# Transposing q, k and the attention output by DMA instead of identity matmuls, in a kernel of linear attention and an MLP

## The chip, the cores and the metric

The kernel runs on one core of a Trainium2 chip. The metric is the time of one execution on the device in microseconds (us), as the median of several runs. A run more than 1.5% above the fastest of its kernel counts as slow and is left out of comparisons. Ratios of two kernels are the mean time of one kernel's fast runs over that of the other's in the same rounds, so they are not quite the ratio of the medians quoted beside them.

Engine names in the profile: PE is TensorE, PEld its weight loads, DVE VectorE, ACT ScalarE, POOL GpSimd, SP the sync engine whose queue issues most DMAs. A DMA has landed when its data have arrived; landing times count from the issue.

## The reference, cut to what matters

```python
# q, k, v: (8, 8, 576, 64) f32; omega: (128, 64); w_in: (512, 2048); w_out: (2048, 512)
def phi(x):                                   # random features
    h = einsum('bhsd,md->bhsm', x, omega) - sum(x*x)/2
    return exp(h - max(h)) / sqrt(128)
q_p, k_p = phi(q * 64**-0.25), phi(k * 64**-0.25)
kv  = einsum('bhsm,bhsd->bhmd', k_p, v);  z = sum(k_p, axis=s)
att = (q_p @ kv) / (q_p @ z + 1e-6)
x   = att.transpose(0, 2, 1, 3).reshape(4608, 512)
h   = x @ w_in;  g = h * clip(h + 3, 0, 6) / 6;  out = g @ w_out
```

## The kernel before

One batch of attention is four pairs of heads. For each pair, q, k and v (288 KB each) are loaded as f32, q and k are cast to bf16 on POOL, and side by side they give 9 blocks of 128x128 that this kernel transposes, so that the head dimension, over which its K and Q matmuls contract, lies on partitions. The kernel before does it with a matmul against an identity and an eviction from PSUM:

```python
def e_T(E, cs=cs, vT=vT):                     # 4 blocks = one unit; 9 units per batch
    for i, c in enumerate(cs):
        src = qkb[(b * NP + c // NR) % 3][:, c % NR, :, :].rearrange("p t d -> p (t d)")
        ins = E.matmul(ring.t[vT.slot][:, 128*i:128*i+128], src, ident[:], start=True, stop=True)
    return ins
...                                           # eviction on DVE or ACT into qkT, then K and Q matmuls
op("POOL", 1.3, lambda E: E.tensor_tensor(    # v scaled by 1/max, both head halves on POOL
    vbd[u2][p0:p1, :, f0:f0 + 64], v32[u3][p0:p1, :, :], cbc, ALU.mult), ...)
...                                           # kv and num matmuls, then xb = num / den
def e_x(E):                                   # the attention output, transposed in the same way
    for t_ in range(4):
        ins = E.matmul(ring.t[vx.slot][:, 128*t_:128*t_+128], xb[pb][:, pr, 128*t_:128*t_+128],
                       ident[:], start=True, stop=True)
    return ins
...                                           # eviction into xT; e_S does the same for 64 left-over rows per batch, into xS
```

The MLP then takes blocks of 512 tokens: `mm1` (xT by wi, 64 matmuls of 512 columns a block, then the activation on ACT and DVE) and `mm2` (by wo, 64 matmuls). Attention of batch b runs while PE does mm1 of block b-1 and mm2 of block b-2.

All instructions go through a small list scheduler that runs when the program is built. It has a cost in us for each operation and fixes the order on every engine. At run time each engine works through its own list in order and waits on semaphores; an instruction that waits holds everything behind it on that engine (in `dma_only` below, a cast on POOL waits 4.70 us and the v scaling listed behind it starts only after it).

The softmax here doesn't subtract the row's maximum and nothing guards it: scores larger than these inputs give would overflow.

## Time and profile before

The time was 363.59 us (363.31 to 364.85). The span of the profiled run, 361.9 us, divides as follows; a block starts where the timeline of PEld shows its first weight load of mm1 (the first of each 64).

| stretch of before | from, us | to, us | length, us |
|---|---|---|---|
| head, to the first matmul of mm1 | 0 | 35.7 | 35.7 |
| blocks 0 and 1 | 35.7 | 97.0 | 61.3 |
| blocks 2 to 6, five periods of 38.2 | 97.0 | 287.9 | 190.9 |
| tail, MLP alone | 287.9 | 361.9 | 74.0 |

These are the groups of the page that the change removes or moves. The columns are line, engine, operation, output from input, shape, count, then busy us and mean ns of one, then idle time of the engine just before them and what ended it.

```profile
L462 POOL TENSOR_TENSOR vbd<-v,cc 64x576 bf16<-64x576 f32 x64 | 73.7, 1152 | 45.0 <-DVE cc L457 30.6
L401 PE MATMUL p<-ident,qkb 128*128 128x128 bf16 x288 | 28.6, 231 | 4.3 <-POOL qkb L379 3.7
L319 ACT CAST qkT<-p 128x512 bf16<-128x512 f32 x41 | 24.1, 590 | 14.0 <-PE p L401 13.4
```

The head and one period as windows (from, to and length in us; busy us and count of PE, PEld, DVE, ACT, POOL; granted clock, DMA share, GB/s). The DMA share adds up packet times over 16 engines and can pass 1 (1.03 in the first row):

```profile
0.00:35.70 35.70, 22.41 (x227) 16.22 (x228) 21.59 (x47) 19.76 (x38) 26.28 (x43) 0.90 1.03 298
135.20:173.40 38.20, 38.14 (x307) 21.54 (x306) 25.49 (x47) 25.36 (x47) 16.30 (x24) 1.00 0.44 121
```

The v scaling on POOL takes 1.15 us for a half.

### The profile page before, as it was taken

To read this page: it belongs to the slowest core of one execution; us is meant where nothing else is said; L and a number is where in the kernel's file an instruction comes from. 1 tells how busy PE (TensorE), PEld (TensorE's weight loads), DVE (VectorE), ACT (ScalarE), POOL (GpSimd) and SP (SyncE) were. 2 spreads that over 40 slices of the span, in tenths; PEclk is the share of its full clock that TensorE was granted. 3 is DMA by queue.
4 is the path that set the end of the run, shared out by engine and by line. 5 is a ranking of instruction groups with operands and counts; after the bars stand their busy time and mean duration, and the time that the engine had idled before them with its cause. 6 is when DMAs were issued, how large, how long until landed. Compare 5 with 4: busy or idle time off the path is not lost.

```text
span 361.9 us, 6522 instructions
## 1 busy us (share of the span) xinstructions
PE 342.1 (95%) x2569; PEld 189.3 (52%) x2569; DVE 222.0 (61%) x406; ACT 211.2 (58%) x383; POOL 137.4 (38%) x206
## 2 busy tenths in 40 slices
PE   3677998999999999999999999999999999999994
PEld 2545565456555655565556555655555544444442
DVE  3676997588558655776567656865687534333411
ACT  3684985575476747584767657674867443444400
POOL 3897596346026621663056505570344100000000
PEclk9898999999999999999999999999999999999999
DMA  7999699635234531645155513322110121121123
GB/s 254 346 279 309 158 223 240 200 95 161 72 94 127 168 115 37 187 130 159 31 145 175 161 29 99 92 55 70 31 29 2 31 58 29 31 54 33 31 60 85
DMA packets 23981, 42.39 MB, mean 117 GB/s; under 512 B 2960, under 2 KB 7056, under 8 KB 23952
## 3 DMA queue, kind: packets, MB, share of 16 engines
q1 hardware_dynamic: 19728, 37.79, 35.8%
q0 software_dynamic: 4224, 4.19, 7.2%
q8 instruction: 20, 0.33, 0.4%
q14 instruction: 9, 0.07, 0.1%
HBM read 36.73 MB, written 9.44 MB: 128 GB/s over the span
## 4 chain that ended last, share of the span: by engine, by line
PE 80%; POOL 11%; DVE 3%; ACT 2%; issue 1%; DMA 1%; SPq 0%; POOLq 0%
PE p L556 32%; PE p L532 30%; POOL vbd L462 7%; PE p L473 4%; PE p L416 4%; PE p L401 4%; PE p L411 3%; PE p L488 2%; POOL qkb L379 2%; PE p L507 1%; DVE mx L429 1%; ACT kp L422 1%; POOL vbd L465 1%; DMA qk<-in_k_dram 1%; ACT qpT L425 1%
## 5 line engine op out<-in xcount | busy, mean ns | idle before, releaser
L539 DVE SCALAR_TENSOR_TENSOR gT<-tsb,p 128x512 bf16<-128x512 bf16 x144 | 98.6, 685 | 80.3 <-ACT tsb L537 78.5
L556 PE MATMUL p<-wo,gT 128*128 128x512 bf16 x576 | 145.2, 379 | 0.5 <-ACT kp L422 0.5
L537 ACT ACTIVATE tsb<-p 128x512 bf16<-128x512 f32 x144 | 86.3, 599 | 89.3 <-PE p L532 89.1
L532 PE MATMUL p<-xT,wi 128*128 128x512 bf16 x512 | 130.4, 379 | 0.1
L462 POOL TENSOR_TENSOR vbd<-v,cc 64x576 bf16<-64x576 f32 x64 | 73.7, 1152 | 45.0 <-DVE cc L457 30.6
L556 PEld LDWEIGHTS p<-wo,gT 128*128 128x128 bf16 x576 | 54.6, 98 | 57.6 <-ACT kp L422 0.7
L379 POOL CAST qkb<-qk 128x576 bf16<-128x576 f32 x64 | 42.7, 668 | 87.7 <-PE p L401 80.1
L532 PEld LDWEIGHTS p<-xT,wi 128*128 128x128 bf16 x512 | 47.1, 98 | 45.0 <-DVE gT L539 0.9
L429 DVE TENSOR_REDUCE mx<-kp 128x4 f32<-128x512 bf16 x72 | 49.0, 681 | 8.4 <-ACT kp L422 8.0
L422 ACT ACTIVATE kp<-p 128x512 bf16<-128x512 f32 x72 | 43.0, 598 | 12.7 <-PE p L416 11.9
L425 ACT ACTIVATE qpT<-p 128x512 bf16<-128x512 f32 x72 | 43.1, 599 | 1.0 <-PE p L411 0.3
L401 PE MATMUL p<-ident,qkb 128*128 128x128 bf16 x288 | 28.6, 231 | 4.3 <-POOL qkb L379 3.7
L319 ACT CAST qkT<-p 128x512 bf16<-128x512 f32 x41 | 24.1, 590 | 14.0 <-PE p L401 13.4
L416 PE MATMUL p<-omk,qkT 128*128 128x128 bf16 x288 | 28.8, 224 | 1.7 <-DVE qkT L320 0.9
L401 PEld LDWEIGHTS p<-ident,qkb 128*128 128x128 bf16 x288 | 21.8, 104 | 14.4 <-POOL qkb L379 3.2
L411 PE MATMUL p<-qkT,omq 128*128 128x512 bf16 x72 | 28.3, 393 | 0.0
L473 PE MATMUL p<-vbd,kp 128*128 128x130 bf16 x288 | 23.0, 226 | 4.6 <-POOL vbd L465 3.9
L416 PEld LDWEIGHTS p<-omk,qkT 128*128 128x128 bf16 x288 | 20.2, 100 | 13.5 <-ACT qkT L319 4.4
L500 DVE TENSOR_TENSOR xb<-p,rec 128x640 bf16<-128x640 f32 x32 | 26.2, 819 | 0.3
L320 DVE CAST qkT<-p 128x512 bf16<-128x512 f32 x31 | 21.3, 686 | 6.1 <-PE p L401 6.1
L473 PEld LDWEIGHTS p<-vbd,kp 128*128 128x128 bf16 x288 | 18.5, 100 | 10.6 <-POOL vbd L465 7.3
L319 ACT COPY osb<-p 128x512 f32<-128x512 f32 x31 | 18.3, 589 | 8.5 <-PE p L556 8.5
(35 smaller groups left out, 160.7 us busy)
## 6 DMA issues: line engine op xcount, KB each, us to landing
qk<-in_q_dram SPq DMA_DIRECT2D x32, 288.0 KB, 3.3
qk<-in_k_dram SPq DMA_DIRECT2D x32, 288.0 KB, 3.9
v<-in_v_dram SPq DMA_DIRECT2D x32, 288.0 KB, 3.1
out_dram<-osb SPq DMA_DIRECT2D x72, 128.0 KB, 2.4
wi<-in_moe_w_in_dram POOLq DMA_DIRECT2D x4, 512.0 KB, 11.8
wo<-in_moe_w_out_dram POOLq DMA_DIRECT2D x4, 512.0 KB, 8.2
om<-in_omega_dram SPq DMA_DIRECT2D x1, 32.0 KB, 1.7
```

The costliest lines, as they stand in the source:

```text
L379: op("POOL", 0.65, lambda E, which=which, u3=u3, u2=u2: E.tensor_copy(qkb[u2][:, :, which, :], qk32[u3][:, which, :].rearrange("p (r d) -> ...
L401: ins = E.matmul(ring.t[vT.slot][:, 128 * i:128 * i + 128], src, ident[:], start=True, stop=True)
L416: ins = E.matmul(ring.t[vK.slot][:, 128 * i:128 * i + 128], qkT_r.t[vqk.slot][:, i, :], omk[:], start=True, stop=True)
L422: op("ACT", actt(512), lambda E, u=u, vK=vK: E.activation(kp[pb][:, 4 * u:4 * u + 4, :].rearrange("p c m -> p (c m)"), ring.t[vK.slot], AF ...
L425: op("ACT", actt(512), lambda E, u=u, vQ=vQ: E.activation(qpT[pb][:, :, 4 * u:4 * u + 4, :].rearrange("m h c p -> m c h p"), ring.t[vQ.slo ...
L429: op("DVE", dvet(512), lambda E, u=u: E.reduce_max(mx[pb][:, 4 * u:4 * u + 4], kp[pb][:, 4 * u:4 * u + 4, :], axis=AX.X), pos(u) + 0.03, r ...
L462: op("POOL", 1.3, lambda E, p0=p0, p1=p1, f0=f0, cbc=cbc: E.tensor_tensor(vbd[u2][p0:p1, :, f0:f0 + 64], v32[u3][p0:p1, :, :], cbc, ALU.mu ...
L473: ins = E.matmul(ring.t[vkv.slot][:, 0:130], kp[pb][:, c0 + r, :], vbd[u2][:, r, :], start=(r == 0), stop=(r == NR - 1))
L532: ins = E.matmul(h_ps[hu], wi[:, c, 128 * f:128 * f + 128], xv[:, c, :], start=(c == 0), stop=(c == NJ - 1))
L537: op("ACT", actt(512), lambda E: E.activation(tsb[tu][:], h_ps[hu], AF.Relu, bias=0.5, scale=1.0 / 6.0), t - 0.1, reads=[("h", hu)], write ...
L539: op("DVE", dvet(512), lambda E: E.scalar_tensor_tensor(gT[gu][:, f, :], tsb[tu][:], 1.0, h_ps[hu], ALU.min, ALU.mult), t - 0.1, reads=[(" ...
L556: ins = E.matmul(ring.t[vo.slot], gT[gu][:, f, 128 * tc:128 * tc + 128], wo[:, f, :], start=(f == 0), stop=(f == NF - 1))
```

## The change

The intent is to take work off TensorE, the bound, and give it to DMA engines that are less than half busy in the middle (share 0.44 in the period above). Its core:

```diff
-    qkT_r = Ring([sbt("qkT%d" % u, [128, 4, 128], BF16) for u in range(3)])
+    qkT = [sbt("qkT%d" % u, [128, NR, 128], BF16) for u in range(4)]
...
-                   t0 - 0.2, writes=[(key, u3)], ...)                       # loads of q, k (and v)
+                   t0 - 0.2, reads=[("wi", pr)] if b == 1 else [], writes=[(key, u3)], ...)
...
-                op("POOL", 0.65, lambda E, ...: E.tensor_copy(qkb..., qk32...), ...)
+                op(EV_C, {"POOL": 0.70, "ACT": actt(576), "DVE": dvet(576)}, evac(...), ...)
+            op("SP", 1.0, lambda E, u2=u2: E.dma_start_transpose(
+                qkT[gp % 4][:], qkb[u2][:].rearrange("p r t d -> p (r t d)")), ...)
...
-            op("PE", 4 * mmt(128), e_T, ...)      # and its eviction
...
-            op("POOL", 1.3, ... vbd ...)
+            op(EV_V, {"POOL": 1.3, "DVE": dvet(576)}, ... vbd ...)
...
-        op("PE", 4 * mmt(128), e_x, ...)          # its eviction, e_S and its eviction
+        op("SP", 0.5, lambda E: E.dma_start_transpose(xT[pb][:, pr, :]..., xb[pb][:, pr, 0:512]), ...)
+        op("SP", 0.2, lambda E: E.dma_start_transpose(
+            xS[:, pr:pr + 1, 64 * b:64 * b + 64], xb[pb][0:64, pr, 512:640]), ...)
...
+    EV_C = ("POOL", "ACT", "DVE")
+    EV_V = ("POOL", "DVE")
```

Besides, the Q matmuls are cut at pair borders, the order of the num matmuls is changed, the weights wait for one more v load, two of the scheduler's costs change (a q or k load from 1.0 to 0.9 us, a cast on POOL from 0.65 to 0.70), and its model gets one DMA clock per issuing engine instead of one for all.

More of the change, by code (lines that the diff above doesn't have):

```diff
@@ L92, in schedule @@
         free = {e: 0.0 for e in engines}
-        dma_free = [0.0]
+        dma_free = {}
         def add(o):
@@ L156, in schedule @@
                 free[e] = st + 0.06
-                dma_free[0] = max(dma_free[0], st + 0.06) + occ
-                o.end = dma_free[0]
+                dma_free[e] = max(dma_free.get(e, 0.0), st + 0.06) + occ
+                o.end = dma_free[e]
             else:
@@ L350, in weights @@
                 w_in[:, 512 * g:512 * g + 512].rearrange("(c p) f -> p c f", p=128)),
-               -0.6 + 0.1 * g, reads=[("v32", min(g + 1, 3))], writes=[("wi", g)], group="dwi%d" % g, inc=16, lat=2.0)
+               -0.6 + 0.1 * g, reads=[("v32", min(g + 2, 3))], writes=[("wi", g)], group="dwi%d" % g, inc=16, lat=2.0)
         else:
@@ L371, in load @@
             for which, src, key in ((0, q, "q32"), (1, k, "k32")):
-                op("SP", 1.0, lambda E, which=which, src=src, u3=u3, pr=pr: E.dma_start(
+                op("SP", 0.9, lambda E, which=which, src=src, u3=u3, pr=pr: E.dma_start(
                     qk32[u3][:, which, :], src[b, 2 * pr:2 * pr + 2].rearrange("h (p r) d -> (h p) (r d)", r=NR)),
-                   t0 - 0.2, writes=[(key, u3)], group="d%s%d" % (key, u3), inc=16, lat=2.0)
+                   t0 - 0.2, reads=[("wi", pr)] if b == 1 else [], writes=[(key, u3)], group="d%s%d" % (key, u3), inc=16, lat=2.0)
             op("SP", 1.0, lambda E, u3=u3, pr=pr: E.dma_start(
                 v32[u3][:], v[b, 2 * pr:2 * pr + 2].rearrange("h (p r) d -> (h p) r d", r=NR)),
-               t0 - 0.1, writes=[("v32", u3)], group="dv32%d" % u3, inc=16, lat=2.0)
+               t0 - 0.1, reads=[("wi", pr)] if b == 1 else [], writes=[("v32", u3)], group="dv32%d" % u3, inc=16, lat=2.0)
             for which, key in ((0, "q32"), (1, "k32")):
-                op("POOL", 0.65, lambda E, which=which, u3=u3, u2=u2: E.tensor_copy(
-                    qkb[u2][:, :, which, :], qk32[u3][:, which, :].rearrange("p (r d) -> p r d", d=D)),
+                op(EV_C, {"POOL": 0.70, "ACT": actt(576), "DVE": dvet(576)},
+                   evac(lambda which=which, u2=u2: qkb[u2][:, :, which, :],
+                        lambda which=which, u3=u3: qk32[u3][:, which, :].rearrange("p (r d) -> p r d", d=D)),
                    t0 - 0.05, reads=[(key, u3)], writes=[("qkb", u2, which)], lat=0.15)
+            op("SP", 1.0, lambda E, u2=u2: E.dma_start_transpose(
+                qkT[gp % 4][:], qkb[u2][:].rearrange("p r t d -> p (r t d)")),
+               t0 - 0.05, reads=[("qkb", u2, 0), ("qkb", u2, 1)], writes=[("qkT", gp % 4)], group="dqkT%d" % (gp % 4), inc=16,
+               lat=2.0)
         for u in range(NU):
@@ L394, in attention @@
             prs = sorted(set(c // NR for c in cs))
-            qb = [("qkb", (b * NP + p) % 3, w) for p in prs for w in (0, 1)]
-            vT, vQ, vK, vqk = Virt(ring), Virt(ring), Virt(ring), Virt(qkT_r)
-            def e_T(E, cs=cs, vT=vT):
-                for i, c in enumerate(cs):
-                    src = qkb[(b * NP + c // NR) % 3][:, c % NR, :, :].rearrange("p t d -> p (t d)")
-                    ins = E.matmul(ring.t[vT.slot][:, 128 * i:128 * i + 128], src, ident[:], start=True, stop=True)
-                return ins
@@ L404, in attention @@
-            op("PE", 4 * mmt(128), e_T, pos(u), reads=qb + ["ident"], writes=[vT, vqk], alloc=[vT, vqk], lat=0.25,
-               name="T%d.%d" % (b, u))
-            op(EV_T, both(512), evac(lambda vqk=vqk: qkT_r.t[vqk.slot][:].rearrange("p c t -> p (c t)"),
-                                     lambda vT=vT: ring.t[vT.slot]),
-               pos(u), reads=[vT], writes=[vqk], name="Tev%d.%d" % (b, u))
-            def e_Q(E, vQ=vQ, vqk=vqk):
-                return E.matmul(ring.t[vQ.slot], omq[:], qkT_r.t[vqk.slot][:].rearrange("p c t -> p (c t)"),
-                                start=True, stop=True)
@@ L414, in e_K @@
-            def e_K(E, vK=vK, vqk=vqk):
-                for i in range(4):
-                    ins = E.matmul(ring.t[vK.slot][:, 128 * i:128 * i + 128], qkT_r.t[vqk.slot][:, i, :], omk[:],
+            qT = [("qkT", (b * NP + p) % 4) for p in prs]
+            runs = []
+            for i, c in enumerate(cs):
+                if runs and runs[-1][0] == c // NR:
+                    runs[-1][3] += 1
+                else:
+                    runs.append([c // NR, c % NR, i, 1])
+            vQ, vK = Virt(ring), Virt(ring)
@@ L417, in e_K, with e_Q @@
+            def e_Q(E, vQ=vQ, runs=runs):
+                for p, r, i, n in runs:
+                    ins = E.matmul(ring.t[vQ.slot][:, 128 * i:128 * (i + n)], omq[:],
+                                   qkT[(b * NP + p) % 4][:, r:r + n, :].rearrange("p c t -> p (c t)"),
                                    start=True, stop=True)
                 return ins
-            op("PE", 4 * mmt(128), e_K, pos(u) + 0.02, reads=[vqk, "omk", "omkz"], writes=[vK], alloc=[vK], lat=0.25)
-            op("PE", mmt(512), e_Q, pos(u) + 0.021, reads=[vqk, "omq", "omqz"], writes=[vQ], alloc=[vQ], lat=0.25)
+            def e_K(E, vK=vK, cs=cs):
+                for i, c in enumerate(cs):
+                    ins = E.matmul(ring.t[vK.slot][:, 128 * i:128 * i + 128],
+                                   qkT[(b * NP + c // NR) % 4][:, c % NR, :], omk[:], start=True, stop=True)
+                return ins
@@ L422, in attention @@
+            op("PE", 4 * mmt(128), e_K, pos(u) + 0.02, reads=qT + ["omk", "omkz"], writes=[vK], alloc=[vK], lat=0.25)
+            op("PE", mmt(512), e_Q, pos(u) + 0.021, reads=qT + ["omq", "omqz"], writes=[vQ], alloc=[vQ], lat=0.25)
             op("ACT", actt(512), lambda E, u=u, vK=vK: E.activation(
@@ L434, in attention @@
                     pair(b, pr, pos(u) + 0.04)
-        sS = b // 2
-        vxs = Virt(ring)
-        def e_S(E):
-            for j in range(NJ):
-                ins = E.matmul(ring.t[vxs.slot][:, 64 * j:64 * j + 64], xb[pb][:, j, 512:640], ident[:, 0:64],
-                               start=True, stop=True)
-            return ins
-        op("PE", 4 * 0.054, e_S, pos(9.5) + 0.08, reads=[("xb", pb, j) for j in range(NJ)] + ["ident"], writes=[vxs],
-           alloc=[vxs], lat=0.25)
-        op(EV_T, both(256), evac(lambda: xS[:, :, 64 * b:64 * b + 64],
-                                 lambda: ring.t[vxs.slot][:, 0:256].rearrange("p (j t) -> p j t", j=NJ)),
-           pos(9.5) + 0.08, reads=[vxs], writes=[("xS", b)])
     def pair(b, pr, t):
@@ L461, in pair @@
             cbc = bass.AP(cc[pb], p0 * NP * NR + c0, [[NP * NR, 64], [1, NR], [0, D]])
-            op("POOL", 1.3, lambda E, p0=p0, p1=p1, f0=f0, cbc=cbc: E.tensor_tensor(
+            op(EV_V, {"POOL": 1.3, "DVE": dvet(576)}, lambda E, p0=p0, p1=p1, f0=f0, cbc=cbc: E.tensor_tensor(
                 vbd[u2][p0:p1, :, f0:f0 + 64], v32[u3][p0:p1, :, :], cbc, ALU.mult), t,
@@ L483, in e_num @@
         def e_num(E):
-            for t_ in range(5):
-                for hh in range(2):
-                    i = 2 * t_ + hh
+            for hh in range(2):
+                for t_ in range(5):
                     c = c0 + rs[t_]
-                    ins = E.matmul(num_ps[:, i // 5, 65 * (i % 5):65 * (i % 5) + 65],
+                    ins = E.matmul(num_ps[:, hh, 65 * t_:65 * t_ + 65],
                                    qpT[pb][:, hh, c:c + 2, :].rearrange("m c p -> m (c p)"),
@@ L500, in pair @@
         op("DVE", dvet(640), lambda E: E.tensor_tensor(
-            xb[pb][:, pr, :].rearrange("p (a i d) -> p a i d", a=2, d=64), nv[:, :, :, 0:64], rbc, ALU.mult),
+            xb[pb][:, pr, :].rearrange("p (i a d) -> p a i d", a=2, d=64), nv[:, :, :, 0:64], rbc, ALU.mult),
            t + 0.01, reads=["num", ("rec", u2)], writes=[("xb", pb, pr)])
-        vx = Virt(ring)
-        def e_x(E):
-            for t_ in range(4):
-                ins = E.matmul(ring.t[vx.slot][:, 128 * t_:128 * t_ + 128], xb[pb][:, pr, 128 * t_:128 * t_ + 128],
-                               ident[:], start=True, stop=True)
-            return ins
-        op("PE", 4 * mmt(128), e_x, t + 0.03, reads=[("xb", pb, pr), "ident"], writes=[vx], alloc=[vx], lat=0.25)
-        op(EV_T, both(512), evac(lambda: xT[pb][:, pr, :], lambda: ring.t[vx.slot]), t + 0.03, reads=[vx],
-           writes=[("xT", pb, pr)])
+        op("SP", 0.5, lambda E: E.dma_start_transpose(xT[pb][:, pr, :].rearrange("p (t k) -> p t k", t=4),
+                                                      xb[pb][:, pr, 0:512]),
+           t + 0.03, reads=[("xb", pb, pr)], writes=[("xT", pb, pr)], group="dxT%d_%d" % (pb, pr), inc=16, lat=2.0)
+        op("SP", 0.2, lambda E: E.dma_start_transpose(
+            xS[:, pr:pr + 1, 64 * b:64 * b + 64], xb[pb][0:64, pr, 512:640]),
+           t + 0.031, reads=[("xb", pb, pr)], writes=[("xS", b, pr)], group="dxS%d_%d" % (pb, pr), inc=16, lat=2.0)
     hcount = [0]
@@ L525, in mm1 @@
         else:
-            xk = [("xS", b) for b in range(B)]
+            xk = [("xS", b, j) for b in range(B) for j in range(NJ)]
             xv = xS
@@ L571, in mm2 @@
                reads=[("osb", ou)], writes=[("out", b, r)], group="dout%d_%d" % (ou, hf), inc=16, lat=2.0)
-    EV_T = ("DVE", "ACT")
+    EV_C = ("POOL", "ACT", "DVE")
+    EV_V = ("POOL", "DVE")
     EV_K = ("DVE", "ACT")
```

## The prediction

> **What bounds the kernel now.** I read the totals of the page first, then the chain of work that ended last, then the busy time by window, then the timeline of one period, and last what the DMA issues cost.
>
> ```profile
> PE 342.1 (95%) x2569; PEld 189.3 (52%) x2569; DVE 222.0 (61%) x406; ACT 211.2 (58%) x383; POOL 137.4 (38%) x206
> PE 80%; POOL 11%; DVE 3%; ACT 2%; issue 1%; DMA 1%; SPq 0%; POOLq 0%
> ```
>
> PE is on 80% of the chain; the only other engine of weight is POOL, at 11%. The windows say where each counts (columns: length, busy us and count of PE, PEld, DVE, ACT, POOL, then clock, DMA share, GB/s):
>
> ```profile
> 0.00:29.90 29.90, 17.00 (x166) 11.78 (x166) 17.31 (x37) 16.56 (x31) 22.19 (x37) 0.93 1.01 293
> 29.90:55.40 25.50, 24.88 (x238) 16.18 (x239) 22.32 (x43) 20.28 (x40) 19.00 (x30) 0.95 0.92 220
> 55.40:93.50 38.10, 36.72 (x300) 20.67 (x299) 27.35 (x51) 21.52 (x38) 18.67 (x26) 1.00 0.62 175
> 164.20:202.40 38.20, 38.14 (x311) 21.55 (x308) 25.50 (x47) 25.36 (x47) 16.33 (x25) 1.00 0.42 121
> 280.00:362.00 82.00, 77.28 (x382) 35.56 (x380) 29.77 (x45) 28.30 (x48) 1.54 (x3) 0.99 0.20 45
> ```
>
> There are three stretches. A head up to about 55 us (attention of batches 0 and 1, first MLP block): POOL is busy 22 of 30 us and DMA is full. A middle of six equal periods of 38.2 us, each with one batch of attention, one block of the first product and one of the second: PE never stops, the other engines are at 67% or below, DMA at 42%. A tail of some 80 us, matmuls of the MLP alone.
>
> Modelled matmul durations overlap, so I take costs from start to start in the timeline of a period:
>
> ```profile
> 159.65 0.39 PE L416 MATMUL p<-omk,qkT 128*128 128x128 bf16 x4
> 159.87 0.38 PE L411 MATMUL p<-qkT,omq 128*128 128x512 bf16 x1
> 160.09 0.39 PE L401 MATMUL p<-ident,qkb 128*128 128x128 bf16 x4
> 160.31 1.03 PE L532 MATMUL p<-xT,wi 128*128 128x512 bf16 x4
> ```
>
> Four 128-column matmuls take 160.31 - 160.09 = 0.22 us, so a group of four transposes costs 0.22 us of PE although the table of groups gives one 231 ns. One of 512 columns takes 0.22 us too (160.09 - 159.87), and the chain gives four of them as 0.86 us. In the same way nine kv matmuls take 0.53 us, ten of num 0.31, four of x 0.22, four of xS 0.12. One period: 32 groups of MLP x 0.864 = 27.64; T 9 x 0.22 = 1.98; K 1.98; Q 9 x 0.216 = 1.94; kv 2.12; num 1.24; x 0.88; xS 0.12. Sum 37.9 us against 38.2 measured: the middle is PE throughput, with 0.3 us of gaps.
>
> [...]this trace shows 55 ns of throughput per transpose on PE[...]; plain loads landed as in
>
> ```profile
> qk<-in_q_dram SPq DMA_DIRECT2D x32, 288.0 KB, 3.3
> out_dram<-osb SPq DMA_DIRECT2D x72, 128.0 KB, 2.4
> POOL qkb L379 <- PE p L401: 80.1, 11, 13.4
> SPq L372 <- POOL qkb L379: 83.1, 48, 9.0
> ```
>
> [...] this trace's SP queue shows 0.33 to 0.43 us per load[...] (In the last lines above, POOL's casts waited 80 us for PE to free the bf16 buffer and the SP queue's loads 83 us for the casts: prefetch is far ahead and has slack.)
>
> **The change part by part.**
> 1. PE loses T (36 matmuls), x (16) and xS (4) of each batch: 1.98 + 0.88 + 0.12 = 2.98 us. Q is cut at pair borders, more instructions but the same columns, about 0. K, kv, num are the same. A period becomes 37.9 - 3.0 = 34.9, with gaps 35.2. Six periods: 6 x 2.98 = **17.9 us** on the path. The other two batches' 6 us lie in the head, where PE is not the bound.
> 2. ACT and DVE lose the evictions: qkT 24.1 + 21.3, xT 11.2 + 8.9, xS 3.3 = 68.8 us, 8.6 per batch. They may take up casts (8 per batch, about 0.65) and v scaling (8, about 0.7): at most 10.7. Together they have 50.9 of 76.4 us in a period now and would have at most 53 of 70: never the bound. In the middle this is worth nothing by itself.
> 3. POOL has 4.1 us of work per pair (2 casts x 0.67, 2 scalings x 1.155, 2 copies x 0.22), which holds 23 + 11 + 4% of the first 60 us of the chain. Sharing it shortens the head. Against this stand a transpose with some 2.5 to 4 us of latency in place of matmul plus eviction (5.67 to 7.02, 1.4 us), and DMA at a share of 1.01 that must now also move 1.8 MB of transposes per batch. The loads of batch 1 wait for the weights, which lets block 0 start earlier. The lowest head I can build from the pieces (batch 0 loaded by 14 us, weights 12 us later, batch 1 another 12 us, then some 8 us of its chain) is about 47; I take **4 us** saved out of the 8 that this would give.
> 4. DMA per batch: 4 x 288 KB + 4 x 128 KB + 4 x 16 KB = 1.77 MB. [...] The scheduler can have qkT a whole batch ahead (four buffers), so its latency is hidden in the middle; xT of the last pair has some us until the next block needs it.
> 5. SP's queue now: 12 loads x 0.33-0.43 + 8 stores x 0.59 = 9 to 10 us per batch. [...] The tail is untouched.
> Sum: 363.6 - 17.9 - 4 = **341.7**. I put the prediction at 343 for small stalls of PE, whose static order is planned on a transposed tile landing in about 3 us.
>
> **Rivals.**
> (a) The SP sequencer becomes the bound. [...] PE waits at K and first-product matmuls and the period stays at about 38, so the time is 355 to 372. [...] For it: [...] a queue that issues in order, where one late transpose holds back loads and stores behind it. Against it: [...] the queue now is busy only a quarter of the time.
> (b) The DMA engines become the bound. [...] Then the middle saves little and the head, full already, grows by 5 to 10 us: 360 to 385. For it: the head's share of 1.01. Against it: the 42% in the middle.
> (c) The head's gain fails: batch 0 waits on transposes in series with loads, and the load waits for weights hold the SP queue while transposes stand behind them. Middle as predicted: 345 to 352.
> (d) The head gains all it can, 8 to 10 us, because POOL was its bound: 335 to 338.
>
> **Range and chances.** The removed PE work is sure and, in a stretch with 0.3 us of gaps, worth its full length if nothing replaces it. I give the main case with (c) and (d) 62%, all faster than 356. Rivals (a) in its mild form and (b) share about 25%, half of them within 2%[...]. So faster 0.63, same 0.13, slower 0.24. The range 331 to 385 leaves out the tail of bad cases and almost nothing below.
>
> **What would show it.** Right: PE 24 us of real work less; the period of the middle (start of a block to the start of the next) 35.2 instead of 38.2 us, PE at 99% there; transposes landing in 2.5 to 5 us; the SP queue busy under 80% of a period; the first matmul of the second product at 47 to 55 us instead of 55.4. Wrong by (a): SP issues of transposes of 4 us or more, back to back, and PE's idle time ended by the transposes with DMA engines half idle. Wrong by (b): DMA share near 1 in the middle and landing times of 8 us or more, loads too. Wrong by (c): a period of 35.2 but a head of 58 us or longer.

The sum came to 341.7 us (363.6 - 17.9 - 4). The 2.5 to 4 us of latency in part 3 was an estimate; over the whole run of the result the median landings are 2.4 us (xS), 3.1 (xT) and 4.4 (qkT).

## More of the kernel before

The weights (wi, wo) are loaded with a cast by DMAs from POOL, on another DMA queue than SP's (in the page, software_dynamic with 4,224 packets and 4.19 MB beside hardware_dynamic with 19,728 and 37.79).

The 288 transposing matmuls waited 4.3 us in all, so the data path in front of them was in time.

## The result

The changed kernel took 399.48 us (399.14 to 399.63), 1.098 times the time before (95% interval 1.093 to 1.102): 36 us slower where 20 us faster was predicted. The profiled span was 397.3 us. First the totals and the shares of the chain that ended last, from the page of the changed kernel:

```profile
PE 324.7 (82%) x2104; PEld 168.7 (42%) x2145; DVE 223.9 (56%) x387; ACT 191.9 (48%) x354; POOL 95.7 (24%) x142
PE 50%; DMA 20%; DVE 9%; POOL 8%; ACT 4%; issue 3%; SPq 2%; POOLq 0%
```

PE's share of the chain fell from 80% to 50%, and DMA rose from 1% to 20%. The windows of the changed kernel, cut at its block starts (same columns as in the prediction):

```profile
0.00:68.30 68.30, 20.07 (x173) 14.57 (x176) 24.80 (x48) 18.95 (x37) 25.51 (x41) 0.80 1.16 227
68.30:102.20 33.90, 28.81 (x201) 15.17 (x205) 24.62 (x44) 21.58 (x42) 11.92 (x18) 0.90 1.15 259
135.30:174.00 38.70, 35.32 (x247) 18.54 (x253) 25.84 (x45) 22.68 (x43) 10.63 (x15) 1.00 0.71 165
250.10:287.20 37.10, 35.39 (x249) 18.71 (x253) 25.43 (x46) 21.49 (x40) 9.31 (x13) 1.00 0.51 109
324.20:397.00 72.80, 68.30 (x312) 30.91 (x316) 24.84 (x37) 23.97 (x41) 0.00 (x0) 0.99 0.21 48
```

| stretch | before, us | after, us | difference | 
|---|---|---|---|
| head, to the first matmul of mm1 | 35.7 | 68.3 | +32.6 |
| blocks 0 and 1 | 61.3 | 67.0 | +5.7 |
| blocks 2 to 6 | 190.9 | 188.9 | -2.0 |
| tail | 74.0 | 73.1 | -0.9 |
| span | 361.9 | 397.3 | +35.4 |

So nearly the whole loss is in the head, where PE is busy 20 of 68 us while the DMA engines are full (share 1.16), and the middle gains next to nothing: its periods are 38.7, 39.1, 37.1, 37.1 and 37.1 us in place of 38.2, and not 35.2.

What PE and the cast engines wait for, from the groups of the changed kernel:

```profile
L450 POOL TENSOR_TENSOR vbd<-v,cc 64x576 bf16<-64x576 f32 x32 | 51.0, 1594 | 158.0 <-DVE cc L445 157.7
L418 PE MATMUL p<-omk,qkT 128*128 128x128 bf16 x288 | 31.2, 237 | 37.7 <-DMA qkT<-qkb 37.7
L461 PE MATMUL p<-vbd,kp 128*128 128x130 bf16 x288 | 23.7, 229 | 16.8 <-POOL vbd L453 14.3
L319 ACT CAST qkb<-qk 128x576 bf16<-128x576 f32 x20 | 13.2, 672 | 16.6 <-DMA qkT<-qkb 12.9
```

The K matmuls waited 37.7 us for the q/k transposes, where before the transposing matmuls waited 4.3 us. Casts wait too (37.4 us on DVE, 21.2 on POOL, 12.9 on ACT): a buffer of bf16 q and k is free only when the transpose that reads it has landed. And POOL's halves of the v scaling take 1,594 ns instead of 1,152 now that DVE does the other half (1,149 in `pool_only` below, where POOL has both halves again).

How the head looks on the chain of the changed kernel (start us, length us, what):

```profile
19.48 12.37 DMA qk<-in_k_dram
...
41.48 12.70 DMA qkT<-qkb
...
63.15 5.11 DMA xT<-xb
```

The first is a load for batch 1: its cast stood in DVE's list before work of batch 0. The second is also batch 1's; the third is the last pair of batch 0. In the timeline, that last pair:

```profile
44.11 0.82 DVE L487 TENSOR_TENSOR xb<-p,rec 128x640 bf16<-128x640 f32 x1
...
56.52 5.96 SPq L383 DMA_TRANSPOSE qkT<-qkb  x1
...
62.53 0.58 SPq L372 DMA_DIRECT2D qk<-in_k_dram  x1
63.15 1.20 SPq L490 DMA_TRANSPOSE xT<-xb  x1
```

The attention output of the last pair was ready at 44.9 us, but SP's in-order queue reached its transpose at 63.15, behind a q/k transpose of batch 1 that held the queue for 6 us and a load. (The time of an SP entry can include a wait; the profile does not divide it.) Mm1 started when it had landed, at 68.3. Before, the last output was ready at 34.0 us and mm1 started at 35.7. So of the 32.6 us, 11 were lost before the last output was ready, 18 while it waited for its turn on SP, and 5 in landing, where 1.7 us had been enough. In those 18 us SP also worked off six loads and the transposes of two earlier pairs of batch 0, which were late behind another q/k transpose of batch 1 (issued at 41.48, 4.1 us).

The median landing times over the whole run look harmless, because the head is a small part of the counts:

```profile
qkT<-qkb SPq DMA_TRANSPOSE x32, 4.4
xT<-xb SPq DMA_TRANSPOSE x32, 3.1
```

Where the queues are quiet that is right: the fastest qkT of the run landed in 3.19 us, the fastest xS (16 KB) in 2.33 us, so the other 272 KB took 0.86 us, an estimate of 324 GB/s. In the head, the first four qkT took 7.1, 8.0, 8.4 and 13.9 us and the first three xT 8.7, 12.2 and 12.6 us.

### The profile page after: what moved, and what is told of

It is laid out like the page before. It is cut to its first block, busy times and chain, and to the rows that moved or that the text cites. A ratio compares the mean times of both kernels' runs of the same rounds, so it can differ in the third digit from the quotient of the medians.

```text
span 397.3 us, 5694 instructions
## 1 busy us (share of the span) xinstructions
PE 324.7 (82%) x2104; PEld 168.7 (42%) x2145; DVE 223.9 (56%) x387; ACT 191.9 (48%) x354; POOL 95.7 (24%) x142
## 2 busy tenths in 40 slices
DMA packets 82348, 56.52 MB, mean 142 GB/s; under 512 B 61328, under 2 KB 65424, under 8 KB 82320
## 4 chain that ended last, share of the span: by engine, by line
PE 50%; DMA 20%; DVE 9%; POOL 8%; ACT 4%; issue 3%; SPq 2%; POOLq 0%
PE p L514 22%; PE p L538 21%; DMA qkT<-qkb 13%; POOL vbd L450 6%; PE p L461 4%; DVE mx L431 3%; DMA xT<-xb 3%; DMA qk<-in_k_dram 3%; DVE gT L521 2%; ACT tsb L519 2%; PE p L475 2%; POOL vbd L453 2%; SPq L383 1%; PE p L418 1%; PE p L411 1%
## 5 line engine op out<-in xcount | busy, mean ns | idle before, releaser
L538 PE MATMUL p<-wo,gT 128*128 128x512 bf16 x563 | 141.9, 379 | 0.8
L450 POOL TENSOR_TENSOR vbd<-v,cc 64x576 bf16<-64x576 f32 x32 | 51.0, 1594 | 158.0 <-DVE cc L445 157.7
L418 PE MATMUL p<-omk,qkT 128*128 128x128 bf16 x288 | 31.2, 237 | 37.7 <-DMA qkT<-qkb 37.7
L418 PEld LDWEIGHTS p<-omk,qkT 128*128 128x128 bf16 x288 | 23.1, 106 | 51.5 <-DMA qkT<-qkb 28.0
L461 PE MATMUL p<-vbd,kp 128*128 128x130 bf16 x288 | 23.7, 229 | 16.8 <-POOL vbd L453 14.3
L320 DVE CAST qkb<-qk 128x576 bf16<-128x576 f32 x12 | 9.0, 753 | 45.4 <-DMA qkT<-qkb 37.4
L320 POOL CAST qkb<-qk 128x576 bf16<-128x576 f32 x32 | 22.3, 698 | 50.1 <-DMA qkT<-qkb 21.2
L411 PE MATMUL p<-qkT,omq 128*128 128x512 bf16 (+3 forms) x92 | 28.6, 356 | 0.3 <-ACT qpT L427 0.2
L450 DVE TENSOR_TENSOR vbd<-v,cc 64x576 bf16<-64x576 f32 x32 | 25.5, 797 | 1.0
L319 ACT CAST qkb<-qk 128x576 bf16<-128x576 f32 x20 | 13.2, 672 | 16.6 <-DMA qkT<-qkb 12.9
L475 PE MATMUL p<-kvz,qpT 128*128 128x65 bf16 x320 | 16.0, 199 | 5.1 <-ACT kvz L319 3.3
```

Of the source, the lines that this page charges most:

```text
L319: return E.copy(dst(), src())
L411: ins = E.matmul(ring.t[vQ.slot][:, 128 * i:128 * (i + n)], omq[:], qkT[(b * NP + p) % 4][:, r:r + n, :].rearrange("p c t -> p (c t)"), st ...
L418: ins = E.matmul(ring.t[vK.slot][:, 128 * i:128 * i + 128], qkT[(b * NP + c // NR) % 4][:, c % NR, :], omk[:], start=True, stop=True)
L450: op(EV_V, {"POOL": 1.3, "DVE": dvet(576)}, lambda E, p0=p0, p1=p1, f0=f0, cbc=cbc: E.tensor_tensor(vbd[u2][p0:p1, :, f0:f0 + 64], v32[u3] ...
L461: ins = E.matmul(ring.t[vkv.slot][:, 0:130], kp[pb][:, c0 + r, :], vbd[u2][:, r, :], start=(r == 0), stop=(r == NR - 1))
L538: ins = E.matmul(ring.t[vo.slot], gT[gu][:, f, 128 * tc:128 * tc + 128], wo[:, f, :], start=(f == 0), stop=(f == NF - 1))
```

## The experiments

Theories after the result. **Q**: a transpose stands on the chain of the head and waits in DMA queues that loads and weights keep full. **W**: the new order of loads (batch 1 waits for weights) is to blame. **C**: the freedom of casts and scaling is to blame. **B** (for the middle): casts wait for transposes to free their buffer and, in an in-order engine, hold the v scaling behind them.

I made one file with a switch per batch between TensorE and DMA transposes, otherwise the changed kernel with casts and scaling on POOL alone and the load order of before:

```diff
+    QK_DMA = ...          # batches whose q and k are transposed by DMA
+    X_DMA = ...           # batches whose attention output is
-    EV_C = ("POOL", "ACT", "DVE")
+    EV_C = ("POOL",)
-    EV_V = ("POOL", "DVE")
+    EV_V = ("POOL",)
-    reads=[("wi", pr)] if b == 1 else [],
-    reads=[("v32", min(g + 2, 3))]
+    reads=[("v32", min(g + 1, 3))]
```

In the tables below "head" is the first weight load of mm1 and "periods" are blocks 2 to 6. Unless it is said otherwise, results are correct. Periods and landings are those of the one profiled run; for `dma_only`, `pool_only` and `late3_cal_xs` that was the slowest of the kernel's runs, for `late3_q3` the fastest.

### One half of the transposes at a time

`none`: `QK_DMA = X_DMA = ()`. `x_only`: `X_DMA` all. `qk_only`: `QK_DMA` all. `dma_only`: both all (built from the changed file itself, without the switch).

> Control: the changed file with every transpose back on TensorE, casts and v scaling on POOL alone, and the loads of batch 1 not waiting for weights. What stays of the change is the planner's cost constants and the order of the num matmuls. All theories: the time of the kernel before, 363.6 us within 2% (358 to 370), first matmul of the first product at 34 to 38 us, period 38.2 us.

> As the control, but x and xS are transposed by DMA (xT and xS, 144 KB per pair), q and k stay on TensorE. Theory Q (a transpose waits in the DMA queues behind loads and weights while the head keeps them full): xT of batch 0 lands 5 to 12 us after its issue, so the first matmul of the first product comes at 42 to 50 us instead of 36; the period falls by about 1.0 us; total 364 to 375 us. Rivals that blame the engine freedom of the casts (C) or the weight waits (W) expect no loss here: head 36 us, period 37.2, total 356 to 359.

> As the control, but q and k are transposed by DMA (288 KB per pair) and x stays on TensorE. Theory Q: qkT of batch 0 lands 7 to 14 us after its issue, as in the changed kernel, first matmul of the first product at 48 to 62 us; period down by up to 2.0 us; total 370 to 390. Rivals C and W: head as before (36 to 38 us), period 36.2 to 37, total 350 to 358.

> All transposes by DMA, but casts and v scaling on POOL alone and no waits of batch 1 loads for weights (both other parts of the change undone). Theory Q: nearly as slow as the changed kernel, 388 to 410 us, with the first matmul of the first product at 60 to 75 us. Rival C or W: most of the 36 us loss is gone, 345 to 368 us.

| run | time, us | ratio to before | head, us | periods, us |
|---|---|---|---|---|
| none | 368.92 | 1.015 | 36.6 | 38.2 all |
| x_only | 371.02 | 1.020 | 52.7 | 36.9, 37.0, 36.9, 37.0, 37.4 |
| qk_only | 380.35 | 1.048 | 62.9 | 36.3, 36.3, 36.3, 36.3, 36.1 |
| dma_only | 395.29 | 1.088 | 69.5 | 40.5, 39.7, 37.2, 34.9, 34.9 |

The control is 1.5% slower than before (its blocks 0 and 1 take 65.6 us instead of 61.3), so some 5 us go with what it keeps of the change besides the transposes: the planner's costs and DMA clocks and the order of num. Each half of the transposes lengthens the head by itself, by 16 and 26 us, and both together by 33; the first two heads, 52.7 and 62.9, lie just outside the expected 42 to 50 and 48 to 62. A part of a longer head comes back, since attention of batch 1 gets ahead meanwhile: in `x_only` blocks 0 and 1 take 58.3 us instead of 65.6, in `qk_only` 60.3. `x_only` also shows a landing on the chain with little waiting for SP: the last output was ready at 36.9 us, its transpose was issued at 40.4 and landed 12.2 us later. Each half shortens the periods by about what it takes off PE: 1.2 us for x (1.0 worked out), 1.9 for q and k (1.98 worked out). With both, the last two periods are 34.9 us, a full 3.3 us less. The first two are longer than before.

### The two other parts of the change

`pool_only` is the changed kernel with `EV_C` and `EV_V` set to POOL alone; `no_wi_wait` is the changed kernel with the waits for `("wi", pr)` and the step `g + 2` taken back.

> The changed kernel with casts and v scaling on POOL alone, nothing else undone. If the shared scaling (POOL's halves took 1.59 us on average beside DVE's, 1.155 alone) and casts that wait in ACT's and DVE's queues are what keeps the last three middle periods at 37.1 us, those fall to 34.9 to 35.3 here; head 66 to 75 us; total 388 to 397.

> The changed kernel with the loads of batch 1 not waiting for weights and the weights one step earlier, nothing else undone. If the order of the loads caused the long head, the first matmul of the first product comes at 40 to 55 us and the total is 370 to 385. If not (theory Q), head 64 to 75 us, last periods still 37.1, total 394 to 404.

`pool_only`: 397.95 us (two runs, 400.25 and 395.64), ratio 1.094, head 68.2, periods 40.3, 41.3, 37.5, 35.0, 34.9. `no_wi_wait`: 404.29 us, ratio 1.112, head 81.0 (expected 64 to 75), last periods 37.0. So C and W fall as causes of the head: without the engine freedom it is the same, and without the waits for weights it is longer, they help. The engine freedom does show in the middle, in both directions: with it the periods that follow the head are shorter (38.7 and 39.1 against 40.3 and 41.3), and the last two are longer (37.1 against 35.0 and 34.9). I had expected 34.9 to 35.3 in the last three and got it in two. Whether the freedom of the casts or that of the scaling lengthens the late periods was not tested apart.

### Which contention in the head

`loads_act` is `dma_only` with the q, k, v loads issued from ACT. `dma_noW` is `dma_only` with wi and wo set by memsets on DVE, so the result is wrong. `ghost` transposes everything on TensorE and issues the DMA transposes of batches 0 and 1 as well, into tiles that nobody reads (six bf16 buffers).

```diff
-op("SP", 0.9, lambda E, which=...: E.dma_start(qk32...        # loads_act; v likewise
+op("ACT", 0.9, lambda E, which=...: E.dma_start(qk32...
-op("POOL", 4.0, lambda E, g=g: E.dma_start(wi...              # dma_noW; wo likewise
+op("DVE", 1.1, lambda E, g=g: E.memset(wi[:, :, 512 * g:512 * g + 512], 0.03125), ...
```

> As dma_only, but the q, k and v loads are issued from ACT, so that SP's queue holds transposes and output stores alone. Theory Q1 (order: a transpose stands in one queue behind prefetch loads and behind SP's waits): in the head qkT and xT land in 3 to 7 us and the first matmul of the first product comes at 42 to 54 us. Theory Q2 (capacity: the engines are full whatever the order): landings stay at 8 to 15 us and the first matmul at 60 to 72 us.

> Wrong result on purpose: as dma_only, but the weights are set to a constant on DVE (eight short memsets) instead of being loaded, which takes the gpsimd queue's traffic out of the head. Theory Q2 (capacity, the weights' transfers next to the transposes): landings of 3 to 7 us, first matmul of the first product at 36 to 48 us. Theory Q1 (order within SP's own queue): the loads of q, k, v still stand in front of the transposes, so landings of 6 to 10 us and a first matmul at 48 to 60 us.

> Every batch transposes on TensorE, but for batches 0 and 1 the q/k and x transposes by DMA are issued as well, into tiles that nobody reads: their traffic is in the head, the dependency is not. Theory D (the chain of the head waits for transposes to land): head within 5 us of the kernel before (first matmul of the first product at 35 to 41 us), total 362 to 370. Theory T (the transposes take DMA time from loads and weights, which come late): first matmul at 45 to 65 us, total 375 to 395.

`loads_act` took 395.08 us, head 62.9; its first qkT still landed in 15.3 and 15.8 us, its xT of batch 0 in 5.2 to 9.2. Taking the loads out of SP's queue gains 7 us of head and nothing in the total, so loads in front of the transposes are not the main thing (Q1, as I put it, falls). But the transposes still stand in front of each other: the last xT of batch 0 waited 13.8 us behind two q/k transposes of batch 1 (5.3 and 8.9 us on SP), as it waited 14.3 us in `dma_only`. No run changes that order. `dma_noW` took 373.95 us (one run, state unknown), head 47.6. Median landing times of its first 45 us:

```profile
qkT<-qkb SPq DMA_TRANSPOSE x7, 4.7
xT<-xb SPq DMA_TRANSPOSE x4, 3.5
```

against `dma_only` in the same window:

```profile
qkT<-qkb SPq DMA_TRANSPOSE x5, 11.6
```

Without the weights' traffic the landing time falls from 11.6 to 4.7 us and the head from 69.5 to 47.6. Of the 33 us that the transposes add to the head, 22 go with the weights' transfers next to them; the other 11 stay with fast landings. The wait of the last xT for its turn on SP falls with them, from 14.3 to 3.9 us in nearly the same order: the q/k transposes of batch 1 in front of it hold SP for 1.7 and 1.5 us instead of 4.5 and 6.0. (The identity-matmul kernel was not run without weights. Its chain holds 3.2 us of DMA before its first matmul of mm1, so little of the 22 us can be a gain that it would have had too.)

`ghost`: 372.35 us, 8.6 above before's 363.72. I had expected 362 to 370 if only the dependency matters and 375 to 395 if only the traffic does. It lies between: traffic that nobody waits for costs some 9 us (it also holds buffers and SP's queue), about a quarter of the loss; the larger part needs somebody to wait.

### Why a transpose is slow beside the weights

`dma_wlate` is `dma_only` with six bf16 buffers, and the loads of wi wait until the q/k transposes of batch 0 have landed. `w_half` and `w_double` are the same with wi loaded in pieces of 256 and 1024 columns, so that a packet of it has 512 or 2048 bytes in SBUF in place of 1024 (in the queue counts below the mean packet of the weights' queue is about 496, 2,020 and 995 bytes).

```diff
-    -0.6 + 0.1 * g, reads=[("v32", min(g + 1, 3))], writes=[("wi", g)]
+    -0.6 + 0.1 * g, reads=[("qkT", 3)], writes=[("wi", g)]                 # dma_wlate
-    wi[:, :, 512 * g:512 * g + 512], w_in[:, 512 * g:512 * g + 512]...
+    wi[:, :, a:a + W], w_in[:, a:a + W]...                                 # W = 256 or 1024
```

> As dma_q6, but the loads of the first product's weights are issued only after the q/k transposes of batch 0 have landed. Theory Q2 (transposes are slowed by the weights' packets beside them): qkT of batch 0 lands in 4 to 8 us as without weights, the first matmul of the first product comes at 48 to 60 us instead of 71, total 365 to 378. If the head is a sum of bytes whatever the order, the first matmul stays at 65 to 75 us.

> As dma_wlate, with the first product's weights in loads of 256 columns instead of 512: packets of 512 bytes instead of 1024. In dma_wlate the two queues moved equal numbers of packets while both had work (2,061 and 2,073 in one window), transposes at about 35 GB/s beside weights at 155. Theory A (the engines take a packet from each queue in turn, so the transposes' rate follows the size of the other queue's packets): transposes rise to 50 to 75 GB/s there, xT of batch 0 lands in 6 to 10 us instead of 9.7 to 14.4. Theory Bw (shared bandwidth by bytes): rates and landings as in dma_wlate.

> As dma_wlate, with loads of 1024 columns: packets of 2048 bytes. Theory A: transposes at 17 to 24 GB/s beside the weights, xT of batch 0 lands in 14 to 25 us. Theory Bw: as dma_wlate, 9.7 to 14.4 us.

`dma_wlate`: 382.30 us, head 61.5 (six buffers with the old order gave 71.3, below). The first four qkT landed in 7.3, 5.7, 4.6 and 4.6 us, as expected, although plain loads ran beside them. Then wi came, and the xT of batch 0 landed in 9.7, 11.5 and 13.1 us: the contention had moved to the next transposes. The head was 61.5 us, just outside the 48 to 60 expected, and the total 4 us above the 365 to 378.

The counts of the DMA queues tell why. This is the queue view of `dma_wlate` from 44 to 58 us, when both queues had work (packets, MB, share of 16 engines; software_dynamic is POOL's queue with the weights, hardware_dynamic is SP's with transposes and loads):

```profile
q0 software_dynamic: 2061, 2.05, 85.9%
q1 hardware_dynamic: 2073, 0.95, 35.2%
```

Of `w_half` from 40 to 46 us:

```profile
q0 software_dynamic: 1452, 0.72, 92.7%
q1 hardware_dynamic: 1113, 0.51, 47.0%
```

Of `w_double` from 30 to 42 us:

```profile
q0 software_dynamic: 1000, 2.02, 91.9%
q1 hardware_dynamic: 917, 0.51, 20.7%
```

While the weights' packets grow fourfold, the two queues move about as many packets as each other (1.3 to 1 at most): it looks as if the engines take one from each in turn. A transpose is made of very small packets. The changed kernel moves 58,368 more packets under 512 bytes than the one before (61,328 - 2,960), 1,824 per pair. One pair has 1,152 + 512 + 64 = 1,728 rows of 128 bf16 values, 256 bytes each, and the single packet records of the trace show just these: 6,912 packets of 256 bytes from 135.3 to 174.0 us, 1,728 for each of four pairs; the other small ones have 4 bytes. So each 256 bytes of a transpose would wait for a packet of the weights. If that is so, larger weight packets must make transposes slower:

| packets of wi | first three xT landings, us |
|---|---|
| 512 B (`w_half`) | 6.9, 8.8, 9.1 |
| 1024 B (`dma_wlate`) | 9.7, 11.5, 13.1 |
| 2048 B (`w_double`) | 11.3, 15.4, 17.5 |

They do, in order, which a share by bytes does not explain. Little else changed: the planner counts 0.8 us per load in `w_half` and `w_double` and 4.0 in `dma_wlate`, but SP's list is the same in all three up to the third xT, and those are issued at 33.8 to 37.4 us. The size of the effect is not what theory A gave. In the three windows the 256-byte packets moved at 36, 32 and 15 GB/s by their records (512, 1024 and 2048 bytes; I had put `dma_wlate` at 35), where I had expected 50 to 75 for `w_half` and 17 to 24 for `w_double`, and the first landing of `w_double`, 11.3, is below the expected 14. The totals hardly differ (385.27, 382.30, 383.54 us, the first and last one run each, state unknown): smaller packets of wi alone do not repair the head. In `w_half` the fourth xT was issued at 44.5 us and took 15.2 us beside wo, whose packets had stayed at 1 KB; in `w_double` it landed in 5.0 us, but SP issued it only at 56.4.

### The middle

`dma_q6` is `dma_only` with six bf16 q/k buffers in place of three.

```diff
-    qkb = [sbt("qkb%d" % u, [128, NR, 2, D], BF16) for u in range(3)]
+    qkb = [sbt("qkb%d" % u, [128, NR, 2, D], BF16) for u in range(6)]
```

> As dma_only, with six bf16 q/k buffers in place of three. In dma_only a cast on POOL waits for the transpose that last read its buffer to land, and POOL's in-order queue holds the v scaling behind it; PE then waits about 3 us at kv in the periods of 40 us. Theory B (this buffer wait is what keeps the middle from its gain): all middle periods 34.9 to 35.6 us, head unchanged within 4 us (69 us to the first matmul of the first product), total 378 to 388. If the buffers are not the cause, periods stay at 37 to 40 and the total at 393 to 397.

The wait it aims at, in the timeline of `dma_only`, for POOL (the bracket is POOL's idle time before the row):

```profile
157.04 0.22 POOL L453 CAST vbd<-cc 64x9 bf16<-64x9 f32 x1
161.96 1.39 POOL L320 CAST qkb<-qk 128x576 bf16<-128x576 f32 x2 [4.70 <-issue]
163.48 1.14 POOL L450 TENSOR_TENSOR vbd<-v,cc 64x576 bf16<-64x576 f32 x1
```

and for PE:

```profile
166.48 0.70 PE L461 MATMUL p<-vbd,kp 128*128 128x130 bf16 x9 [2.98 <-POOL vbd L453]
```

The transpose of the pair that had used this buffer was issued at 157.62 and landed 4.2 us later, at 161.8; only then could POOL cast into it, with the v scaling behind the cast, and PE stood 2.98 us at kv. (The profile names no releaser for the cast; the times and the order of buffers give it.) With six buffers: 388.69 us, ratio 1.067, head 71.3, periods 39.6, 37.8, 34.9, 34.9, 34.9. So theory B holds for one more period and 7 us; two periods stayed long, and the total just missed the expected range. The trace shows the same wait again in the first of them: with six buffers POOL had cast further ahead, and its cast at 158.21 waited 4.8 us for a transpose that was issued at 152.80 and landed at 158.10; PE stood 3.1 us at kv. More buffers do not help where the transposes themselves are issued late.

### Keeping DMA transposes out of the head

`late` transposes batches 0 and 1 on TensorE and 2 to 7 by DMA, with six buffers and the planner's constants of before. `late3` begins with batch 3. `late3_q3` is `late3` with three buffers.

```diff
+    QK_DMA = (2, 3, 4, 5, 6, 7)     # late; (3, 4, 5, 6, 7) in late3
+    X_DMA = (2, 3, 4, 5, 6, 7)
```

> Batches 0 and 1 transpose on TensorE as in the kernel before, batches 2 to 7 by DMA; six bf16 q/k buffers, POOL alone for casts and v scaling, the planner's constants of the kernel before. Theory Q plus B: the head is as before (first matmul of the first product near 36 us, third block near 95 to 99), five to six periods of about 35 us in place of 38.2: 343 to 350 us, faster than both kernels. If DMA transposes cost PE time in the middle too, periods stay at 37 to 40 and the total is 358 to 372.

> As late, but the DMA transposes begin with batch 3 instead of 2: in late the transposes of batch 2 were issued at 45 to 64 us, beside the last loads and weights of the head, landed 11 to 16 us later, and block 2 began at 113 us instead of 97. Theory Q: block 2 begins at 95 to 99 us as before, five periods of 34.9 us follow, tail 73 us: 343 to 350 us, 4 to 6% faster than before. If DMA transposes have another cost of their own, 354 to 362.

> late3 with three bf16 q/k buffers instead of six. Theory B (casts wait for the transposes to free their buffer, and hold the scaling behind them): two or more of the five periods 36 to 40 us, total 4 to 12 us above late3. Rival: the buffers do not matter once the head is over, total within 2 us of late3.

| run | time, us | ratio to before | head, us | periods, us |
|---|---|---|---|---|
| late | 358.94 | 0.988 | 36.6 | 30.6, 34.7, 34.9, 35.0, 34.8 |
| late3 | 355.35 | 0.978 | 34.8 | 37.0, 39.0, 35.1, 34.9, 34.8 |
| late3_q3 | 360.35 | 0.992 | 35.6 | 39.9, 39.8, 36.0, 35.0, 34.9 |

The head is back and the times are below before's, though by less than expected each time: `late3` is faster by 2.2% (interval of the ratio 0.975 to 0.980), `late` and `late3_q3` by 1.2 and 0.8%, which counts as the same. Block 2 of `late` does begin at 113.1 us, as I wrote when I expected `late3`, but not because PE stood: it was busy 47.9 of the 48.2 us before, with more of mm2 moved in front. What PE lost in `late` is one wait of 7.7 us, before block 3, for the last xT of that block. In `late3` the periods of 37.0 and 39.0 remain, and three buffers instead of six cost 5 us.

### A plan that knows what SP costs

The scheduler counts 0.06 us of SP for every DMA that it issues. The trace has 1.2 us and more for a transpose, whatever its size, 0.59 for a store, about 0.43 for a load (medians of the changed kernel). `late3_cal` gives it 1.25, 0.58 and 0.45; `late3_cal_xs` also sends xS, four transposes of 16 KB a batch, back to TensorE.

```diff
-                free[e] = st + 0.06
+                hold = 1.25 if o.group[:3] in ("dqk", "dxT", "dxS") else 0.58 if o.group[:4] == "dout" else 0.45
+                free[e] = st + (hold if e == "SP" else 0.06)
-            op("SP", 0.2, lambda E: E.dma_start_transpose(xS...          # late3_cal_xs only
+            # e_S and its eviction, as in the kernel before
```

> As late3, but the planner counts the time that SP needs to issue: 1.25 us per transpose, 0.58 per store, 0.45 per load, in place of 0.06 for all. Theory P (the static order is wrong because the plan thinks that SP's queue is free): the two periods of 37 and 39 us become 34.9 to 36, total 346 to 351. Rival S (SP's queue is too full whatever the order): 353 to 358 as late3.

> As late3_cal, but xS goes back to TensorE: per batch 0.12 us more of PE, one eviction of 0.42 us, and four transposes of 1.23 us less on SP's queue. Rival S: periods 35.0 to 35.5 only here, total 346 to 351 and at least 3 us below late3_cal. Theory P: within 2 us of late3_cal.

`late3_cal`: 352.97 us, ratio 0.970, periods 37.7, 35.2, 34.7, 34.9, 35.4. `late3_cal_xs`: 349.77 us, ratio 0.961 (95% interval 0.958 to 0.963), periods 35.3, 35.5, 35.0, 35.0, 35.5. Both theories have a part: the right costs gave 2.4 us (352.97, where theory P expected 346 to 351), the emptier queue another 3.2. This version is 3.9% faster than the kernel before and 12% below the changed one. Its windows:

```profile
0.00:36.40 36.40, 22.58 (x224) 16.60 (x228) 21.99 (x47) 20.04 (x38) 26.21 (x43) 0.86 1.03 295
100.90:136.20 35.30, 34.18 (x246) 18.28 (x249) 22.52 (x41) 19.85 (x39) 16.26 (x24) 1.00 0.74 190
171.70:206.70 35.00, 34.74 (x252) 18.91 (x257) 22.14 (x41) 21.48 (x39) 13.61 (x20) 1.00 0.50 113
```

The head is that of the kernel before, and PE is busy 34.7 of 35.0 us in a period that was 38.2.

## Why the prediction was wrong

Up to the start of block 2 the prediction's sum had 7 us less (4 of the head and one of its six periods) and the trace has 38 us more; in blocks 2 to 6 it had 14.9 us less and the trace has 2.0; in the tail nothing, and the trace has 0.9 less. So 45 of the 57 us between the sum, 341.7, and the result lie before block 2.

**Step 1, the work taken off PE.** Right in size. A period without stalls is 34.9 us, the very number of the sum, in `dma_only`, `dma_q6`, `late3` and others. The count was not: from block start to block start there are five periods of 38.2 us, not six, and batch 2's attention lies in the 31.4 us of block 1; the window 55.40:93.50 that was read as the first period already shows DVE busy 72% and a DMA share of 0.62. And wrong in one half-sentence: "worth its full length if nothing replaces it". In the changed kernel something did: five periods gained 2.0 us in all instead of 14.9. I named PE's static order as a cause for "small stalls"; the runs show a buffer wait that casts hand on to the v scaling (`dma_only`, `late3_q3`), something in the sharing of casts and scaling that `pool_only` undoes (last two periods 35.0 and 34.9 us instead of 37.1; POOL's halves take 1,149 ns instead of 1,594), and a plan that takes SP's time for nothing (`late3_cal`).

**Step 2, ACT and DVE.** Right: neither became the bound. ACT is busy at most 64% of a window of the result, DVE at most 73% (24.6 of 33.9 us, block 0), more than the share expected but with room.

**Step 3, the head. This is the step that failed.** It said "some 2.5 to 4 us of latency in place of matmul plus eviction" and took 4 us as saved. In the head the q/k transposes of batch 0 landed in 7 to 14 us, and from the last attention output of batch 0 to its landed transpose it took 23.3 us, 18.2 of them waiting for a turn on SP and 5.1 landing. The first matmul of mm1 came 32.6 us later; that of mm2, to which the prediction measured its head, at 80.2 us instead of the 47 to 55 that it gave as its sign. I had seen the DMA share of 1.01 there and added the transposes' bytes to it, but used a landing time like that of quiet stretches (3.19 us at best for a qkT) for something that would now stand on the chain. Before, the chain of the head had 3.2 us of DMA, one load; the rest of the traffic did not stand on it.

**Step 4, DMA time.** That it fits in the middle was right: the share of the five periods is 0.71, 0.70, 0.56, 0.51 and 0.21. (The rate that the forecast assumed was shown by no run; the estimate from the landings of 3.19 and 2.33 us above is 324 GB/s.) It does not hold in the head, where landings of 288 KB took 7 to 14 us; without the weights' transfers 22 of the 33 us go away, and the packet counts point to turns taken with their packets.

**Step 5, SP's queue.** The costs of a transpose that I used here were shown by no run. In the timeline the twelve transposes of one middle period take about 17 us, loads and stores another 9, so the queue does fit in a period; but I had the cost rise with size, and it is 1.2 us or more for every one: at least 1.22 us for 16 KB (xS), 1.20 for 128 KB (xT) and 1.28 for 288 KB (qkT), medians 1.23, 1.22 and 1.79, in the changed kernel. The costs of loads (0.33 to 0.43 us) and stores (0.59) I had from the trace of the kernel before. That the queue's time would cost nothing was wrong too: an xT stands behind other entries (18 us in the head), and sending only the small xS back to PE gained 3.2 us.

**The rivals.** Rival (a) had the period right, about 38 us, by luck: SP was in issue 22 to 28 us of each period from block 2 to 5, so it was not the bound that (a) made of it. What it held for itself, that a late transpose holds back what stands behind it, is what happened in the head. Rival (b) had the right place and the right reason (the head, already full), but it gave the head 5 to 10 us, where it was 33, and blamed the middle's capacity, which was there (share 0.71 at most). Rival (c) described SP's queue correctly; the waits for weights that it feared turned out to help. The range, 331 to 385, did not reach the result, because in none of the rivals did full queues lengthen a chain of dependent transfers by this much.

**What stays open.** An order of SP's list in which batch 0's last xT stands before batch 1's q/k transposes was not tried, so how much of the 14 to 18 us of waiting it would save is not known. How the remaining 11 us of the head (the loss that stays without the weights' traffic) divide between landing latency and SP's order was not measured apart. Nor was the reason why the first periods of the changed kernel are shorter than those of `pool_only`.

## What to carry to other kernels

In this kernel a transfer in place of an engine's instruction cost little where it could be issued early (PE busy 34.7 of 35.0 us in a middle period of `late3_cal_xs`), and the whole backlog of the queues, the issuing one included, where its result was awaited (23.3 us for the last xT of batch 0): read the DMA share of the very stretch in which somebody will wait, not of the whole span. Where small packets share the DMA engines with another queue's large ones, as in the head here (2,073 beside 2,061 packets in `dma_wlate`, 0.95 MB beside 2.05), count packets and not only bytes. When work moves to DMA, give the issuing queue's own time to the planner, and check which buffers are now held until a transfer lands.
